# An attention and mixture-of-experts kernel on one Trainium2 core: row stores in four pieces, a weight's quarters further apart, an 80/64 split of the pooled tokens, and an earlier flag

## The chip, the cores and the metric

The kernel runs on one core of one Trainium2 chip. The metric is device time in microseconds of one execution. A core has engines that run side by side, each with its own queue of instructions: TensorE (PE, with its weight loads shown as PEld), VectorE (DVE), ScalarE (ACT), GpSimd (POOL) and SyncE (SP), which here does nothing but issue DMA transfers. An engine takes its instructions in the order in which the program lists them; semaphores make one wait for another.

## The reference

Eight batches, eight heads, 576 tokens, head size 64. Two attentions are added: one over tokens pooled by four (144 of them), whose output is repeated four times, and one over a band of tokens less than four apart. The sum, seen as 4608 rows of 512, goes through a mixture of eight experts: each row goes to the one expert with the largest logit.

```python
q_d = q.reshape(B, H, Sd, factor, D).mean(axis=3)      # k_d, v_d too
out_up = np.repeat(sm_attn(q_d, k_d, v_d), factor, axis=2)
mask = np.abs(pos[:, None] - pos[None, :]) < factor
out_local = softmax(where(mask, scale * q @ k.T, -1e9)) @ v
x = (out_up + out_local).transpose(0, 2, 1, 3).reshape(B * S, H * D)
logits = normalized(x) @ normalized(expert_emb).T / tau
expert_idx = np.argmax(logits, axis=1)
for e in range(E):
    h = np.maximum(x[expert_idx == e] @ w1[e], 0.0)
    out[expert_idx == e] = gate_w[expert_idx == e, None] * (h @ w2[e])
```

## The kernel before, in words

**Attention.** The work is cut into 32 units, each a pair of heads of one batch (four units to a batch). A loop over iterations -2 to 32 (`attention`) goes through a hand-written list of small operations, ORDER, in each iteration; LEAD says for each operation by how many units it runs ahead. In iteration i, k and q of unit i + 2 are transposed (L373), the scores of unit i + 1 are made (its mask matmul is L418, so that the mask of unit u marks iteration u - 1), and unit i is finished: its value matmuls (`op_val`, L522, 36 of them as PE counts) and pooled values (`op_vald`, L509). Unit i - 1 is turned into rows (`op_xr`).

**Pooled values.** The 144 pooled tokens lie on partitions, in two groups CD = (128, 16). `load_v` (L348) loads v for both groups, `op_pv` and `op_vd` (L409, L414, on POOL) add four rows to one, `op_wdT` and `op_adT` bring the pooled attention to the same shape, `op_vald` multiplies the two groups one after the other.

**Loads.** All of them are issued by SP, in program order: k and q for two units at a time (`load`, L342, eight transfers), v for one unit (`load_v`, two), and vw, the overlapping windows of v that the banded attention needs, for two units, a "half" (`load_w`, L357 and L363: two edge transfers, four middle windows, two edge transfers). Half j serves units 2j and 2j + 1; its vw is listed in iteration 2j - 3 and needed in iteration 2j. One half's eight transfers are what the trace shows as L357 x2, L363 x4, L357 x2.

**Weights of the first expert.** `first_weights` is a generator that moves one step in each iteration whose number less one is in W0, just after the place called mid. It loads w1 in four quarters, squares and splits them into two float16 parts on ACT (L857) and DVE (L858), and loads w2's quarters (L877) into the space that w1's quarters leave: a quarter is asked for right after the split that frees its space, in iterations 10, 11, 12 and 13. Squares of w2 follow in iterations 16 to 18, its splits in 20, 21, 23 and 24.

**Rows and places.** When a batch's four units are done, `place` gives functions that run in the following iterations. `store` (at mid, iteration 4b + 5 for batch b) finishes the logits and writes the batch's 576 rows of 520 values to DRAM (`xd`): four tiles of 128 rows in one transfer (L582) and the last 64 rows in another (L583). `most`, `first` and `count` run at the place called tail of that iteration and the next two; they find the expert of each row and its place in that expert's list. For batch 7 all of it comes after the attention. Early gathers (L1111, POOL, in iteration 28) fetch the first three slots of rows from batches 0 to 5; behind them on POOL stands the pooling of v for unit 29 (L414).

**Experts.** Rows are handled in slots of 128. A slot takes 24 matmuls with w1 (L1214 to L1216) and 24 with w2 (L1250 to L1252). `run_slots` interleaves slot q's first half with slot q - 1's second half. Where the next slot has another expert, `renew` splits new weights under a branch on ACT, DVE and POOL; later matmuls wait for that branch, taken or not. `out_rows` (L1259, ACT) scales a slot's result, `store` (L1263, POOL) scatters it. After the last of the 38 fixed slots, `last_slots` loads a flag into a register on every engine (L1091) and branches on it: five more slots are run if the flag is set, and it is not with these inputs.

Of the kernel before, what the change touches and what calls it, by code (L numbers as in the profile page):

```python
# [8 lines left out]
F32 = mybir.dt.float32  # L9
# [13 lines left out]
SD = S // 4  # L23
G, QB = S // 64, 32
WK, WV = QB + 6, 64 + 6
CD = (128, SD - 128)
CP = S // 6
TB = 128
NTB = -(-S // TB)
# [27 lines left out]
MASKED = -1.0e30  # L57
KSC, QSC = 2.0 ** -2, 2.0 ** -5

W0 = (-1, 0, 1, 2, 4, 5, 6, 7, 8, 9, 10, 11, 12, 15, 16, 17, 18, 19, 20, 22, 23)  # L60


class Kern:
# [128 lines left out]
    def attention(self, ctx):  # L192
# [7 lines left out]
        for i in range(2):  # L200
# [3 lines left out]
            self.an.append(z.tile([128, G, WV], F32, name=f"an{i}"))  # L204
            self.sums.append(z.tile([128, G + 3], F32, name=f"sums{i}"))
            self.vw.append(z.tile([WV, G, 4, D], F32, name=f"vw{i}"))
        self.vr = [z.tile([128, 2, 2, 4 * D], F32, name=f"ld_v{i}") for i in range(3)]
        self.lg = z.tile([TB, NTB, E + 1], F32, name="lg")
        self.oh = self.cp.tile([TB, B, NTB + 1, E], BF16, name="oh")
        units = [(b, hp) for b in range(B) for hp in range(NHP)]  # L210
# [32 lines left out]
            nc.vector.memset(self.xT[i][:, S:], 0.0)  # L243
            nc.vector.memset(self.sums[i], 1.0)
        for vr in self.vr:
            nc.gpsimd.memset(vr[:, 1], 0.0)
        next(crows)
        load(1)
        load_v(0)
# [159 lines left out]
        self.nc.gpsimd.tensor_tensor(out=vr[:, :, 0:2 * D], in0=vr[:, :, 0:2 * D], in1=vr[:, :, 2 * D:], op=ALU.add)  # L409

    def op_vd(self, s):
        v, vd = s["v"], self.wk.tile([128, 2, 2, D], F32, name="vd")
        s["vd"] = vd
        self.nc.gpsimd.tensor_tensor(out=vd, in0=v[:, :, :, 0:D], in1=v[:, :, :, D:2 * D], op=ALU.add)  # L414

# [82 lines left out]

    def op_adT(self, s, c):
        if "adT" not in s:  # L500
            s["adT"] = self.wk.tile([128, 2, 2, 3, 48], F32, name="adT", bufs=1)
        self.nc.scalar.activation(out=s["adT"][:CD[c], c].rearrange("p h c j -> p c h j"),
                                  in_=s["wdT", c].rearrange("p c (h j) -> p c h j", h=2), func=AF.Copy)

# [65 lines left out]
    def place(self, b, xr, ls, mid):  # L570

        nc, rt = self.nc, self.rt
        v = nc.vector
        lg, oh = self.lg, self.oh[:, b]
        shp = [TB, NTB, E]

        def bc(x):
            return x.unsqueeze(2).broadcast_to(shp)

        def save(queue):  # L580
            r0 = b * S
            queue.dma_start(out=self.xd[r0:r0 + S - TR].rearrange("(t p) c -> p t c", p=TB), in_=xr[:, :NTB - 1])  # L582
            queue.dma_start(out=self.xd[r0 + S - TR:r0 + S], in_=xr[:TR, NTB - 1])  # L583

        def store():
            pt = self.bank()[:, :NTB * 32].rearrange("p (t e) -> p t e", e=32)
            nc.tensor.transpose(out=pt[:, :NTB - 1], in_=ls[:, :TB], identity=self.ident)
            nc.tensor.transpose(out=pt[:TR, NTB - 1], in_=ls[96:, TB:], identity=self.ident[96:, 96:])
            for ps, ts in ((slice(0, TB), slice(0, NTB - 1)), (slice(0, TR), slice(NTB - 1, NTB))):
                v.tensor_scalar(out=lg[ps, ts, :E], in0=pt[ps, ts, :E], scalar1=self.itau[ps], scalar2=None, op0=ALU.mult)  # L590
            v.tensor_copy(out=xr[:, :, DM:], in_=lg[:, :, :E])
            save(nc.sync)

        def most():

            l8 = lg[:, :, :E]
            mx = s["mx"] = rt.tile([TB, NTB], F32, name="lmx")
            v.reduce_max(out=mx, in_=l8, axis=AX.X)
            v.tensor_tensor(out=l8, in0=l8, in1=bc(mx), op=ALU.is_ge)

        def first():

            l8, mx = lg[:, :, :E], s["mx"]
            v.tensor_tensor(out=l8, in0=l8, in1=self.rev, op=ALU.mult)
            v.reduce_max(out=mx, in_=lg, axis=AX.X)
            v.tensor_tensor(out=oh[:, :NTB], in0=l8, in1=bc(mx), op=ALU.is_equal)

        def count():

            pk = self.bank()[:, :(NTB + 1) * E].rearrange("p (t e) -> p t e", e=E)  # L610
            nc.tensor.matmul(out=pk, lhsT=self.tri, rhs=oh, start=True, stop=False)
            for t in range(1, NTB + 1):
                nc.tensor.matmul(out=pk[:, t:], lhsT=self.onesb, rhs=oh[:, :NTB + 1 - t], start=False,
                                 stop=(t == NTB))
            rk = rt.tile(shp, F32, name="rk")
            pos = s["pos"] = rt.tile([TB, NTB], F32, name="pos")
            v.tensor_tensor(out=rk, in0=pk[:, :NTB], in1=self.base.unsqueeze(1).broadcast_to(shp), op=ALU.add)
            v.tensor_tensor(out=self.base, in0=self.base, in1=pk[:, NTB], op=ALU.add)
            v.tensor_tensor(out=rk, in0=rk, in1=oh[:, :NTB], op=ALU.mult)
            v.reduce_sum(out=pos, in_=rk, axis=AX.X)  # L620

        def divide():

            pos, posi = s["pos"], rt.tile([TB, NTB], I32, name="posi")
            v.tensor_copy(out=posi, in_=pos)
            v.tensor_scalar(out=posi, in0=posi, scalar1=SLOT - 1, scalar2=None, op0=ALU.bitwise_and)
            pm, pb = self.pm[:, b], self.pb[:, b]
            v.tensor_copy(out=pm, in_=posi)
            v.tensor_tensor(out=pb, in0=pos, in1=pm, op=ALU.subtract)
            for t in range(NTB):  # L630
                nc.gpsimd.tensor_scalar(out=self.at[:, b * NTB + t], in0=self.iota, scalar1=pm[:, t:t + 1],
                                        scalar2=None, op0=ALU.is_equal)

        def pick():
            most()
            first()

        def rank():
            count()
            divide()  # L640

        s = {}
        if b == B - 1:
            return [store, pick, rank]
        mid.append(store)
        return [most, first, rank] if b >= BEARLY - 1 else [most, first, count, divide]

# [218 lines left out]
    def first_weights(self):  # L866
# [6 lines left out]
        def get(which, p):  # L873
            w = (self.w1, self.w2)[which][0].rearrange("(c p) f -> p c f", p=128)
            src = self.piece(w, which, p)
            t = flat[:, p].rearrange("p (c f) -> p c f", c=src.shape[1])
            nc.sync.dma_start(out=t, in_=src)  # L877
            return t
# [23 lines left out]
        yield  # L902
        for p in range(NP):
            split(0, p)
            tiles[p] = get(1, p)
            yield
        square(1, 0, 1)
        yield
        square(1, 2)
# [94 lines left out]
        with tc.If(code > 4 if which else code < 1):  # L1004
            self.measure(which)

    def run_slots(self, q0, q1):

        last = q1 - 1
        for q in range(q0, q1):  # L1010
# [50 lines left out]
            self.weigh(q)  # L1061
            if ahead:
                self.turn(q + 2)
            if ps:
                self.out_rows(q - 1, ps)
            if q > q0 + 1:
                self.stage_next(1, b - 1, 1)
            self.gate(q)
            if old:
                self.renew(1, b)  # L1070
            if new:
                self.norms(q + 1)
# [3 lines left out]
            if old:  # L1076
                self.stage_next(1, b, *((0,) if new else (0, 1)))
        self.scale_gate(last)
        self.mm2(last)
        self.store(last)  # L1080

# [6 lines left out]
    def last_slots(self):  # L1088

        q0, q1 = NEARLY + NFIX, NEARLY + NSLOT  # L1090
        more = self.nc.values_load(self.flg[:1, NFIX, 3:4], min_val=0, max_val=1)  # L1091
        with self.tc.If(more > 0):
            for q in range(q0, min(q0 + 4, q1)):
                self.gather(q)
            for b in (NFIX, NFIX + 1):
# [171 lines left out]
    def run(self):  # L1267
# [80 lines left out]
            yield from w1  # L1348

        self.late = late()  # L1350
        self.run_slots(NEARLY, NEARLY + NFIX)
        self.last_slots()


# [43 lines left out]
```

## Time and profile before

| | us |
|---|---|
| three runs | 730.84, 736.08, 740.85 (median 736.08) |
| profiled execution | 733.08 |
| its span, first to last instruction | 731.4 |
| TensorE busy in it | 701.0 |
| VectorE, ScalarE, GpSimd busy | 473.1, 462.0, 443.4 |
| mean granted TensorE clock | 0.988 |

The profile is of one execution. In a timeline row stand the start in us from the span's beginning, the duration, the engine (with a q where it is the engine's sequencer, as for all transfers that SP issues), the line, the operation, what it writes and reads, its shape, how many were merged, and in brackets the idle time ahead of it and what ended that. A row with a source line has shortest, median and longest duration in ns. In a group the number after the bar is the time busy, then the mean of one in ns, then the idle time ahead.

### The profile page before, as it was taken

Reading aid. Unit: us, or ns where it says so; the run is one execution under the profiler, and the core shown is the slowest. Engines: PE = TensorE matmul, PEld = TensorE weight load, DVE = VectorE, ACT = ScalarE, POOL = GpSimd, SP = SyncE. Lnnn points to the kernel's source line nnn. Section 1 sums busy time; section 2 is a strip of 40 time slices with the busy share of each in tenths; the row PEclk is TensorE's granted clock in tenths of the full one; section 3 lists DMA queues with packets and bytes.
Section 4 is the critical chain, followed back from the end, with each engine's and each line's share of the span. In section 5 each row is a group of like instructions: output and inputs, shape, how many; then the busy total and the mean of one; then the engine's idle time right before and its main releaser. Section 6 shows DMA issues by size and latency. Waiting matters only on the chain. (4 is left out here: it accounts for less than half of the span.)

```text
span 731.4 us, 22049 instructions
## 1 busy us (share of the span) xinstructions
PE 701.0 (96%) x7471; PEld 412.9 (56%) x7471; DVE 473.1 (65%) x1415; ACT 462.0 (63%) x1063; POOL 443.4 (61%) x857
## 2 busy tenths in 40 slices
PE   8999999989999989999999999999999999999992
PEld 5777887768878864444444444444444444444440
DVE  6778799958998887576556467565643565366320
ACT  4677788667787664356666577775755555558420
POOL 5865788765878885556564564556466645564420
PEclk9999999989999999999999999999999999999997
DMA  9889889988788976959959988898897599779640
GB/s 162 163 202 193 221 185 234 211 210 213 158 215 185 215 244 129 221 123 248 235 126 250 231 208 216 191 247 193 251 220 132 116 238 216 147 175 202 177 74 19
DMA packets 284117, 138.92 MB, mean 190 GB/s; under 512 B 251186, under 2 KB 260402, under 8 KB 283968
## 3 DMA queue, kind: packets, MB, share of 16 engines
q1 hardware_dynamic: 277248, 118.15, 73.8%
q0 software_dynamic: 6560, 19.03, 8.2%
q8 instruction: 61, 1.00, 0.6%
q14 instruction: 88, 0.72, 0.3%
q10 hardware_dynamic: 160, 0.02, 0.0%
HBM read 213.05 MB, written 20.33 MB: 319 GB/s over the span
## 5 line engine op out<-in xcount | busy, mean ns | idle before, releaser
L1214 PE MATMUL bank<-w1h,xT 128*128 128x512 f16 x328 | 124.3, 379 | 1.4 <-ACTq L995 1.4
L1250 PE MATMUL bank<-w2h,hT 128*128 128x512 f16 x328 | 124.4, 379 | 0.9 <-ACTq L995 0.9
L1215 PE MATMUL bank<-w1l,xT 128*128 128x512 f16 x328 | 124.3, 379 | 0.1
L1252 PE MATMUL bank<-w2h,hT 128*128 128x512 f16 x328 | 124.4, 379 | 0.0
L1251 PE MATMUL bank<-w2l,hT 128*128 128x512 f16 x328 | 124.4, 379 | 0.0
L1216 PE MATMUL bank<-w1h,xT 128*128 128x512 f16 x328 | 124.3, 379 | 0.0
L1111 POOL DMA_INDIRECT xg<-xd,ids x41 | 45.8, 1118 | 79.7 <-POOLq L995 36.9
L1227 ACT ACTIVATE h<-bank 128x512 f16<-128x512 f32 x82 | 48.3, 589 | 58.4 <-PE bank L1216 57.5
L1263 POOL DMA_INDIRECT out_dram<-o,ids x41 | 44.9, 1096 | 50.0 <-ACTq L995 20.0
L380 ACT ACTIVATE kq<-bank 128x288 f32<-128x288 f32 x128 | 48.1, 472 | 38.8 <-PE bank L373 38.4
L833 ACT ACTIVATE junk<-st 128x1024 bf16<-128x1024 f32 (+1 forms) x30 | 67.5, 2251 | 4.6 <-DVE end L734 2.7
L1259 ACT ACTIVATE o<-bank,gt 128x512 f32<-128x512 f32 x41 | 27.8, 677 | 63.5 <-issue 18.7
L409 POOL TENSOR_TENSOR ld_v<-ld_v 128x256 f32<-128x256 f32 x64 | 48.9, 783 | 22.6 <-DMA ld_v<-in_v_dram 22.6
L389 POOL TENSOR_TENSOR pool_kq<-kq 128x288 f32<-128x288 f32 x62 | 45.3, 731 | 25.1 <-ACT kq L380 25.1
L81 POOL TENSOR_SCALAR nw_t<-nw_y,nw_a 128x1 f32<-128x1 f32 x123 | 51.7, 420 | 12.4
L1231 DVE SCALAR_TENSOR_TENSOR h<-bank,h 128x512 f16<-128x512 f32 x82 | 56.3, 688 | 2.7 <-ACTq L1004 2.2
L858 DVE SCALAR_TENSOR_TENSOR w2l<-st,wscl,w2h 128x1024 f16<-128x1024 f32 x32 | 39.6, 1280 | 26.1 <-ACT w2h L857 26.1
L1214 PEld LDWEIGHTS <-xT 128*128 128x128 f16 x328 | 35.1, 107 | 34.5 <-DMA xT<-x 0.5
L1251 PEld LDWEIGHTS <-hT 128*128 128x128 f16 x328 | 32.0, 98 | 39.4 <-issue 1.2
L1250 PEld LDWEIGHTS <-hT 128*128 128x128 f16 x328 | 32.0, 98 | 39.0 <-DMA hT<-h 0.6
L1216 PEld LDWEIGHTS <-xT 128*128 128x128 f16 x328 | 31.9, 97 | 39.1 <-issue 0.4
L1252 PEld LDWEIGHTS <-hT 128*128 128x128 f16 x328 | 32.0, 98 | 38.8
(221 smaller groups left out, 1556.2 us busy)
## 6 DMA issues: line engine op xcount, KB each, us to landing
st<-in_moe_w_dram SPq DMA_DIRECT2D x148, 1024.0 KB
ld_k<-in_k_dram SPq DMA_DIRECT2D x64, 144.0 KB
ld_q<-in_q_dram SPq DMA_DIRECT2D x64, 144.0 KB
xd<-xr SPq DMA_DIRECT2D x8, 1040.0 KB
ld_v<-in_v_dram SPq DMA_DIRECT2D x32, 256.0 KB
st<-in_moe_w_dram SPq DMA_DIRECT2D x16, 512.0 KB
vw<-in_v_dram SPq DMA_DIRECT2D x64, 122.5 KB
vw<-in_v_dram SPq DMA_DIRECT2D x32, 64.0 KB
```

What stands on the lines that cost most here:

```text
L81: g.tensor_scalar(out=t, in0=y, scalar1=y, scalar2=a, op0=ALU.mult, op1=ALU.mult)
L380: self.nc.scalar.activation(out=dst, in_=s["qk", r, w].rearrange("p (m i) -> p i m", m=3), func=AF.Copy, scale=(KSC, QSC)[w])
L409: self.nc.gpsimd.tensor_tensor(out=vr[:, :, 0:2 * D], in0=vr[:, :, 0:2 * D], in1=vr[:, :, 2 * D:], op=ALU.add)
L833: self.nc.scalar.activation(out=junk, in_=src, func=AF.Square, accum_out=acc)
L1214: nc.tensor.matmul(out=ps, lhsT=xT[:, 0, k], rhs=self.w1h[:, k, ns], start=(k == 0), stop=False)
L1215: nc.tensor.matmul(out=ps, lhsT=xT[:, 0, k], rhs=self.w1l[:, k, ns], start=False, stop=False)
L1216: nc.tensor.matmul(out=ps, lhsT=xT[:, 1, k], rhs=self.w1h[:, k, ns], start=False, stop=(k == self.KC - 1))
L1227: self.nc.scalar.activation(out=h2[:, 0], in_=ps, func=AF.Relu)
L1231: self.nc.vector.scalar_tensor_tensor(out=h2[:, 1], in0=ps, scalar=0.0, in1=h2[:, 0], op0=ALU.max, op1=ALU.subtract)
L1250: nc.tensor.matmul(out=ps, lhsT=hh, rhs=self.w2h[:, j, :], start=(j == 0), stop=False)
L1251: nc.tensor.matmul(out=ps, lhsT=hh, rhs=self.w2l[:, j, :], start=False, stop=False)
L1252: nc.tensor.matmul(out=ps, lhsT=hl, rhs=self.w2h[:, j, :], start=False, stop=(j == self.FC - 1))
```

## The change

CD becomes (80, 64); the tiles that hold it have 80 partitions instead of 128. `save` writes only a range of row tiles, always on SP's queue: for batches 0 to 6 tile 0 goes at `store`, tile 1 at `most`, tile 2 at `first`, and tile 3 with the last 64 rows at `count`. Batch 7 is stored as before. w2's quarters are asked for in iterations 10, 12, 13 and 15; its squares come in iterations 17, 19 and 21, its splits in 23 to 26. In the last slot of `run_slots` the renewal of w2 stands ahead of `out_rows` of the slot before. The flag is loaded ahead of the last slot's second half, by a function handed to `run_slots`.

```diff
-CD = (128, SD - 128)
+CD = (80, SD - 80)
...
-W0 = (-1, 0, 1, 2, 4, 5, 6, 7, 8, 9, 10, 11, 12, 15, 16, 17, 18, 19, 20, 22, 23)
+W0 = (-1, 0, 1, 2, 4, 5, 6, 7, 8, 9, 10, 11, 12, 14, 16, 18, 20, 21, 22, 23, 24, 25)
...
-        self.vr = [z.tile([128, 2, 2, 4 * D], F32, name=f"ld_v{i}") for i in range(3)]
+        self.vr = [z.tile([CD[0], 2, 2, 4 * D], F32, name=f"ld_v{i}") for i in range(3)]
...
-            nc.gpsimd.memset(vr[:, 1], 0.0)
+            nc.gpsimd.memset(vr[CD[1]:, 1], 0.0)
...
-        def save(queue):
+        def save(t0, t1):
             r0 = b * S
-            queue.dma_start(out=self.xd[r0:r0 + S - TR].rearrange("(t p) c -> p t c", p=TB), in_=xr[:, :NTB - 1])
-            queue.dma_start(out=self.xd[r0 + S - TR:r0 + S], in_=xr[:TR, NTB - 1])
+            if t0 < NTB - 1:
+                n = min(t1, NTB - 1)
+                nc.sync.dma_start(out=self.xd[r0 + t0 * TB:r0 + n * TB].rearrange("(t p) c -> p t c", p=TB),
+                                  in_=xr[:, t0:n])
+            if t1 == NTB:
+                nc.sync.dma_start(out=self.xd[r0 + S - TR:r0 + S], in_=xr[:TR, NTB - 1])
...
-            save(nc.sync)
+            save(0, 1 if b < B - 1 else NTB)
...
+            if b < B - 1:
+                save(1, 2)
...
+            if b < B - 1:
+                save(2, 3)
...
+            if b < B - 1:
+                save(3, NTB)
...
         for p in range(NP):
             split(0, p)
-            tiles[p] = get(1, p)
+            if p != 1:
+                tiles[max(p - 1, 0)] = get(1, max(p - 1, 0))
             yield
+        tiles[NP - 1] = get(1, NP - 1)
+        yield
...
-    def run_slots(self, q0, q1):
+    def run_slots(self, q0, q1, end=None):
...
+            if old and not new:
+                self.renew(1, b)
             if ps:
                 self.out_rows(q - 1, ps)
...
-            if old:
+            if old and new:
                 self.renew(1, b)
...
         self.scale_gate(last)
+        if end:
+            end()
         self.mm2(last)
...
-        more = self.nc.values_load(self.flg[:1, NFIX, 3:4], min_val=0, max_val=1)
-        with self.tc.If(more > 0):
+        with self.tc.If(self.more > 0):
...
+        def more():
+            self.more = self.nc.values_load(self.flg[:1, NFIX, 3:4], min_val=0, max_val=1)
+
-        self.run_slots(NEARLY, NEARLY + NFIX)
+        self.run_slots(NEARLY, NEARLY + NFIX, more)
```

More of the change, by code (lines that the diff above doesn't have):

```diff
@@ L411, in op_vd @@
     def op_vd(self, s):
-        v, vd = s["v"], self.wk.tile([128, 2, 2, D], F32, name="vd")
+        v, vd = s["v"], self.wk.tile([CD[0], 2, 2, D], F32, name="vd")
         s["vd"] = vd
@@ L500, in op_adT @@
         if "adT" not in s:
-            s["adT"] = self.wk.tile([128, 2, 2, 3, 48], F32, name="adT", bufs=1)
+            s["adT"] = self.wk.tile([CD[0], 2, 2, 3, 48], F32, name="adT", bufs=1)
         self.nc.scalar.activation(out=s["adT"][:CD[c], c].rearrange("p h c j -> p c h j"),
```

## The prediction

> **What bounds the kernel now.** I read the page first, then the busy times by stage, then the rows around the one stage in which TensorE (PE) falls behind, then the end.
>
> ```profile
> span 731.4 us, 22049 instructions
> PE 701.0 (96%) x7471; PEld 412.9 (56%) x7471; DVE 473.1 (65%) x1415; ACT 462.0 (63%) x1063; POOL 443.4 (61%) x857
> ```
> ```profile
> 90.00:140.00 50.00, 49.93 (x1084) 40.13 (x1082) 47.35 (x114) 39.16 (x124) 41.88 (x61) 1.00 0.89 211
> 140.00:160.00 20.00, 16.82 (x319) 13.42 (x318) 12.15 (x31) 13.63 (x42) 12.14 (x22) 0.85 0.94 213
> 160.00:180.00 20.00, 20.00 (x377) 16.02 (x376) 15.77 (x45) 15.38 (x52) 13.92 (x24) 0.98 0.87 198
> 160.00:240.00 80.00, 79.73 (x1666) 64.44 (x1665) 70.25 (x174) 61.64 (x198) 61.26 (x94) 1.00 0.84 193
> ```
>
> PE is the bound: 701 of 731.4 us. The columns of the stages are the stage, its length, then PE, PEld, DVE, ACT and POOL busy, granted clock, DMA share and GB/s. In the attention PE is full in 90:140 and 160:240, but from 140 to 160 it loses 3.2 us, and there alone the clock is under 1. Half speed for 0.15 x 20 / 0.5 = 6.0 us of that stage and 0.02 x 20 / 0.5 = 0.8 us of the next one makes 6.8 us. The mask matmul, one per unit (a pair of heads of a batch), gives the price:
>
> ```profile
> 145.33 0.31 PE L418 MATMUL bank<-mask,identb 128*128 128x342 bf16 x1
> 157.96 0.49 PE L418 MATMUL bank<-mask,identb 128*128 128x342 bf16 x1
> 167.10 0.31 PE L418 MATMUL bank<-mask,identb 128*128 128x342 bf16 x1
> 237.23 0.31 PE L418 MATMUL bank<-mask,identb 128*128 128x342 bf16 x1
> ```
>
> The nine units from 167.10 to 237.23 take 70.13 / 9 = 7.79 us each; the two before take 12.63 and 9.14. So the stall costs 12.63 + 9.14 - 15.58 = **6.2 us**, about half of it idle time and half the half clock behind it. What ends it is the load of vw, the windows of v:
>
> ```profile
> 143.58 0.57 SPq L582 DMA_DIRECT2D xd<-xr  x1
> 144.19 2.13 SPq L583 DMA_DIRECT2D xd<-xr  x1
> 146.42 0.61 SPq L877 DMA_DIRECT2D st<-in_moe_w_dram  x1
> 147.13 1.12 SPq L357 DMA_DIRECT2D vw<-in_v_dram  x2
> 148.30 4.25 SPq L363 DMA_DIRECT2D vw<-in_v_dram  x4
> 152.65 0.63 SPq L357 DMA_DIRECT2D vw<-in_v_dram  x1
> 213.26 2.93 SPq L363 DMA_DIRECT2D vw<-in_v_dram  x4
> ```
> ```profile
> 149.95 0.86 PE L509 MATMUL bank<-adT,vd 128*64 128x144 f32 x8 [0.61 <-ACT adT L502]
> 153.34 0.56 PE L522 MATMUL bank<-aT,vw 70*64 70x64 f32 x6 [1.95 <-DMA vw<-in_v_dram]
> ```
>
> Batch 2's store (L582, L583), the last quarter of w2 (L877) and the vw load for units 16 and 17 ("half 8") stand one behind the other on SP's queue. SP goes from one transfer to the next with some 0.05 us between them, so it is never ahead: a load is issued when SP gets to it. That is the second bound of this stage.
>
> **The change, part by part.**
>
> *Store in pieces, quarters apart.* The large transfer of a store carries four of a batch's four and a half row tiles:
>
> ```profile
> xd<-xr SPq DMA_DIRECT2D x8, 1040.0 KB
> ```
>
> So batch 2's store put 1040 x 4.5 / 4 = 1170 KB on the queue ahead of half 8's load, and the four quarters of w2 had been asked for in four units running. Afterwards 520 KB of the store and three quarters stand ahead of it, and all of both ahead of half 9's load. Bytes and descriptors are the same in the end, so what counts is how much earlier SP gets through, and how much room PE has behind it. Room is read from vw loads: SP's last issue of one, its landing, and the matmuls that need it.
>
> ```profile
> 86.02 1.15 SPq L357 DMA_DIRECT2D vw<-in_v_dram  x2
> 184.80 1.41 SPq L357 DMA_DIRECT2D vw<-in_v_dram  x2
> 216.28 1.15 SPq L357 DMA_DIRECT2D vw<-in_v_dram  x2
> ```
> ```profile
> 88.71 0.34 PE L522 MATMUL bank<-aT,vw 70*64 70x64 f32 x4 [0.42 <-DMA vw<-in_v_dram]
> 187.81 1.27 PE L522 MATMUL bank<-aT,vw 70*64 70x64 f32 x36
> 219.29 1.27 PE L522 MATMUL bank<-aT,vw 70*64 70x64 f32 x36
> ```
>
> Half 4 waited until 88.71 for a transfer whose issue ended at 87.17: landing takes 1.54 us. The last four of a unit's 36 value matmuls need it, some 1.0 us behind the first. Half 10 (SP done at 186.21, landed 187.75, needed 188.8) has 1.1 us of room, half 12 (217.43, 218.97, 220.3) has 1.3. So even with the stall gone PE cannot come more than about 1.1 us earlier through the later units, unless SP does. SP comes earlier by what the burst cost it: L583 took 2.13 us where its other rows have 0.52 (below), and half 8's four middle windows 4.25 where half 12's took 2.93, of which I take 1.0: together 2.6 us.
>
> Against that, each batch has five transfers instead of two, three more for SP.
>
> ```profile
> L583 SPq DMA_DIRECT2D xd<-xr x8: 514/519/2130, 79.6 to 282.8; - x8
> ```
>
> One more costs SP between 0 (it fills a pause that SP would have had anyway, such as the 2.13 here) and 0.52 + 0.06 = 0.58 us. DMA engines are busy 0.84 to 0.94, which argues for pauses, but SP has no gap even at 0.84, which argues for the full price; I take 0.25, a little under the middle. Ahead of half 10 stand three more transfers for each of batches 0 to 2, ahead of half 12 those of batch 3 too. Gain at half 10: 1.1 + 2.6 - 9 x 0.25 = 1.45; at half 12: 1.3 + 2.6 - 12 x 0.25 = **0.9 us**, the smaller, which I take. By the ends: 0 gives 3.7, 0.58 gives 3.9 - 7.0 = -3.1. At half 8 itself the need was near 152.4 (153.34 - 1.95 + 1.0) and the landing 153.80 + 1.54 = 155.3: short by 2.9. SP's 2.6 and one quarter fewer (0.5), less 6 x 0.25, leave it short by about 1.3, too little, I think, to halve the clock. The stall is late next at halves 9, 10 and 12, in small pieces.
>
> [...]
>
> *The last piece of batch 5.* Early gathers read batches 0 to 5. Its store was issued in iteration 25; its last piece now stands in iteration 27, just ahead of half 15's load.
>
> ```profile
> 249.63 1.13 SPq L357 DMA_DIRECT2D vw<-in_v_dram  x2
> ```
> ```profile
> 252.98 1.27 POOL L1111 DMA_INDIRECT xg<-xd,ids  x1 [0.73 <-DVE ids L700]
> 257.19 0.74 POOL L414 TENSOR_TENSOR vd<-ld_v 128x256 f32<-128x256 f32 x1
> ```
> ```profile
> 257.99 0.47 PE L509 MATMUL bank<-adT,vd 128*64 128x144 f32 x4
> ```
> ```profile
> DMA to landing us min/median/max: 2.6/4.7/8.0
> ```
>
> Two issues from 249.63 on end near 250.8; landing, by the gathers' own (the row above), takes 2.6 or more, so 253.4 at best and 255.5 by the median. The first gather starts at 252.98. Behind it on POOL stand two gathers and vd of unit 29, done at 257.93, and PE needs that at 257.99: no room. Cost 0.4 to 2.5 us, and more if SP is later; I take **1.0**, towards the low end, as a plain store lands without the gather's reading of ids.
>
> *80 and 64 tokens.* The same number of instructions with the same free size:
>
> ```profile
> L409 POOL TENSOR_TENSOR ld_v<-ld_v 128x256 f32<-128x256 f32 x32 | 25.2, 788 | 22.1 <-DMA ld_v<-in_v_dram 22.1
> L409 POOL TENSOR_TENSOR ld_v<-ld_v 16x256 f32<-16x256 f32 x32 | 24.9, 779 | 0.5 <-DMA ld_v<-in_v_dram 0.5
> ```
>
> 128 and 16 partitions cost 788 and 779 ns, so any split does; bytes stay. Zero.
>
> *w2's squares and splits later.* The last split moves from iteration 24 to 26, the same sixteen instructions.
>
> ```profile
> L858 DVE SCALAR_TENSOR_TENSOR w2l<-st,wscl,w2h 128x1024 f16<-128x1024 f32 x32 | 39.6, 1280 | 26.1 <-ACT w2h L857 26.1
> ```
>
> DVE is busy 70.25 of 80 us in 160:240, with the splits in it; four units running have 1.28 us each where there were two pairs. Between 0 and 0.7 us (two units, 7.79 x 0.88 + 1.28 less 7.79); I take 0, since they lie behind PE's own 7.79.
>
> *The end.* In the last fixed slot the check on w2 stood on ACT behind out_rows, which waits for the slot before.
>
> ```profile
> 710.62 0.38 PE L1251 MATMUL bank<-w2l,hT 128*128 128x512 f16 x1
> 710.84 0.38 PE L1252 MATMUL bank<-w2h,hT 128*128 128x512 f16 x1
> 712.09 0.38 PE L1250 MATMUL bank<-w2h,hT 128*128 128x512 f16 x1 [0.87 <-ACTq L995]
> ```
> ```profile
> 711.30 0.69 ACT L1259 ACTIVATE o<-bank,gt 128x512 f32<-128x512 f32 x1 [4.07 <-issue]
> ```
> ```profile
> L1091 POOLq TENSOR_LOAD <-flg x1: 287/287/287, 718.3 to 718.3; - x1
> ```
>
> PE's matmuls follow each other at 0.22 us, so the last 24 could start at 711.06, not 712.09: **1.03 us**. ACT idles 4.07 us ahead of L1259; the moved check fits there, and without that cover it would cost what it costs now. The flag's load leaves the chain of POOL behind the last store: 0 (if the store's landing sets the end) to 0.29; I take all. On PE it now stands ahead of the last 24 matmuls, hidden by those already queued. Sum at the end: **1.3 us**, bounds 0 and 1.3.
>
> **Sum.** 733.1 (the profiled execution; 731.4 of span and 1.7 around it) - 0.9 + 1.0 + 0 + 0 - 1.3 = 731.9. That execution is 3.0 us under the median of 736.1 and inside the three runs (730.84 to 740.85). What lifts a run above it is, I think, a stall like this one, and smaller bursts make those rarer, so I carry the sum over as it is: **732 us**.
>
> **Rivals.**
> 1. *All of the stall goes and nothing is given back* (0.20): 733.1 - 6.2 - 1.3 = 725.6. For it: 6.2 us stand in one place. Against it: 1.1 us of room at half 10.
> 2. *SP's issue becomes the bound; slower* (0.25): each transfer costs SP its full 0.58 us and vw comes late at every second half: 3.1 later at half 12, 1.0 at the gathers or 3 with SP's lateness, 1.3 won: 733.1 + 2.8 to 4.8, 737. It decides from 12c - 3.9 + 1.0 - 1.3 > 0, c over 0.35 us. For it: SP without gaps. Against it: its pauses.
> 3. *A smaller stall still halves the clock* (0.10): 6.8 / 2 = 3.4 more than my sum, 735.3.
> 4. *The check does not free PE at the end* because another wait ends last there (0.05): 733.2.
>
> **How the numbers follow.** My forecast has 0.40. The range reaches from rival 1, less a little for the runs' spread, to rival 2 with the median's 3 us on top: **724 to 740**. A measurement of this kernel tells about 2% from no change, 721.4 or 750.8; all cases lie inside, so faster 0.05, same 0.92, slower 0.03.
>
> **What would show it.** Right: no unit over 10 us in the mask rows; clock 1.00 in 140:180; waits of L522 on vw in pieces under 1.5 us around halves 9 to 12; L1111 first ended by xd, not ids; the last 24 matmuls without a gap. Wrong: unit 17 still over 12 us; SP with gaps (then the pieces are free, rival 1); or units 18 to 28 over 8.1 us each (rival 2).

## The result, and the profile after

The kernel after takes 742.57 us (median of 20 runs, 739.60 to 748.26), the kernel before on the same chip 734.38 (20 runs, 730.84 to 740.85): a ratio of 1.0107, 95% interval [1.0088, 1.0127]. The change costs some 8 us. It was forecast to gain one; the range ended at 740. The profiled execution of after is its slowest, 748.26, so its single losses are larger than those of a usual run. Losses below are read from profiles, sizes from medians. Runs more than 1.5% above the fastest of their kernel are left out of every ratio; one of 1877.98 us, of the kernel with the ratio 0.9959, is among them.

The head of the page of after, and the busy times of the same stages as before (stage, length, then PE, PEld, DVE, ACT, POOL busy, granted clock, DMA share, GB/s):

```profile
span 746.5 us, 22071 instructions
...
PE 706.2 (95%) x7471; PEld 418.6 (56%) x7471; DVE 471.6 (63%) x1415; ACT 463.4 (62%) x1063; POOL 446.6 (60%) x857
```
```profile
90.00:140.00 50.00, 46.29 (x944) 37.77 (x941) 41.92 (x103) 34.70 (x106) 38.48 (x56) 0.93 0.89 198
140.00:160.00 20.00, 20.00 (x406) 16.10 (x405) 16.58 (x43) 15.02 (x52) 14.85 (x26) 1.00 0.84 187
160.00:180.00 20.00, 13.24 (x257) 10.74 (x255) 9.88 (x24) 9.76 (x29) 11.06 (x18) 0.77 0.80 199
160.00:240.00 80.00, 73.24 (x1514) 59.29 (x1515) 61.37 (x154) 58.30 (x185) 54.52 (x83) 0.94 0.85 197
```

The stage that lost 3.2 us before, 140:160, is now full, at clock 1.00: the stall at half 8 is gone in this execution. In its place PE loses 3.7 us in 90:140 and 6.8 us in 160:180, each with a granted clock of 0.50 from within the wait on, 102.3 to 109.2 and 170.6 to 180.8. The mask rows, one a unit, show the two places, and what PE waited for:

```profile
91.42 0.31 PE L418 MATMUL bank<-mask,identb 128*128 128x342 bf16 x1
103.01 0.45 PE L418 MATMUL bank<-mask,identb 128*128 128x342 bf16 x1 [3.23 <-DVE ls L568]
113.53 0.31 PE L418 MATMUL bank<-mask,identb 128*128 128x342 bf16 x1
...
160.18 0.31 PE L418 MATMUL bank<-mask,identb 128*128 128x342 bf16 x1
175.01 0.44 PE L418 MATMUL bank<-mask,identb 128*128 128x342 bf16 x1 [6.41 <-DVE ls L568]
185.37 0.31 PE L418 MATMUL bank<-mask,identb 128*128 128x342 bf16 x1
```

Units of 11.59 and 10.52 us, 14.83 and 10.36, where 7.79 is usual: (22.11 - 15.58) + (25.19 - 15.58) = 16.1 us. Unit 30, under "Open" at the end of the section on the prediction, loses another 4.2. The DVE copy L568 is not the cause; it waits in its turn, 9.01 us in the second case. ScalarE's timeline has the first engine that stands still:

```profile
102.11 0.28 ACT L554 ACTIVATE xr<-bank 128x128 f32<-128x128 f32 x1 [4.62 <-DMA xd<-xr]
...
174.11 0.28 ACT L554 ACTIVATE xr<-bank 128x128 f32<-128x128 f32 x1 [7.60 <-DMA vw<-in_v_dram]
```

L554 is the first write of a batch's rows, and the row buffer `xr` has two buffers. Batch 2 writes where batch 0's rows lie, batch 4 where batch 2's do. With the store in pieces, the last piece of batch b is listed in iteration 4b + 7, and batch b + 2 writes in 4b + 9. SP runs some two iterations behind the list, as its timeline shows (L584 is the store of whole tiles, L587 that of the last 64 rows):

```profile
96.83 0.62 SPq L584 DMA_DIRECT2D xd<-xr  x1
97.49 0.51 SPq L587 DMA_DIRECT2D xd<-xr  x1
...
167.21 0.57 SPq L887 DMA_DIRECT2D st<-in_moe_w_dram  x1
167.82 0.47 SPq L584 DMA_DIRECT2D xd<-xr  x1
168.33 0.51 SPq L587 DMA_DIRECT2D xd<-xr  x1
```

Batch 0's last piece leaves SP at 98.00 and ScalarE goes on at 102.11, 4.1 us later; batch 2's leaves at 168.84, and ScalarE goes on at 174.11. In the second row the page names a vw transfer, but L554 reads or writes nothing of vw. The trace has the last packet of the store's last two transfers end at 101.36 in the first case and at 173.39 in the second, each shortly ahead of L554. Everything behind L554 on ScalarE, the copies of k and q (L380) among it, waits; then PE, DVE and POOL do.

The end went as forecast. Of the last matmuls with w2 the 24 that stood behind a gap of 0.87 us now follow without one:

```profile
727.27 0.38 PE L1268 MATMUL bank<-w2h,hT 128*128 128x512 f16 x1
727.49 0.38 PE L1266 MATMUL bank<-w2h,hT 128*128 128x512 f16 x1
727.70 0.38 PE L1267 MATMUL bank<-w2l,hT 128*128 128x512 f16 x1
```

From the last unit's mask (277.46) to the end of the span it takes 469.0 us, 470.4 before (731.4 - 261.00). All of the loss stands in the attention.

### The profile page after: what moved, and what is told of

It reads as the page before. It is cut to its first block, busy times and chain, and to the rows that moved or that the text cites. A ratio compares the mean times of both kernels' runs of the same rounds, so it can differ in the third digit from the quotient of the medians.

```text
span 746.5 us, 22071 instructions
## 1 busy us (share of the span) xinstructions
PE 706.2 (95%) x7471; PEld 418.6 (56%) x7471; DVE 471.6 (63%) x1415; ACT 463.4 (62%) x1063; POOL 446.6 (60%) x857
## 5 line engine op out<-in xcount | busy, mean ns | idle before, releaser
L380 ACT ACTIVATE kq<-bank 128x288 f32<-128x288 f32 x128 | 47.8, 474 | 33.8 <-PE bank L373 32.9
L81 POOL TENSOR_SCALAR nw_t<-nw_y,nw_a 128x1 f32<-128x1 f32 x123 | 54.2, 440 | 12.4
L409 POOL TENSOR_TENSOR ld_v<-ld_v 80x256 f32<-80x256 f32 x64 | 50.4, 807 | 15.3 <-DMA ld_v<-in_v_dram 15.3
L491 ACT ACTIVATE aT<-bank 70x384 f32<-70x384 f32 x96 | 43.8, 489 | 18.7 <-PE bank L484 18.3
L1266 PEld LDWEIGHTS <-hT 128*128 128x128 f16 x328 | 32.1, 98 | 40.7 <-DMA hT<-h 2.6
L1268 PEld LDWEIGHTS <-hT 128*128 128x128 f16 x328 | 32.1, 98 | 38.7
```

Source lines behind the costliest of these rows:

```text
L81: g.tensor_scalar(out=t, in0=y, scalar1=y, scalar2=a, op0=ALU.mult, op1=ALU.mult)
L380: self.nc.scalar.activation(out=dst, in_=s["qk", r, w].rearrange("p (m i) -> p i m", m=3), func=AF.Copy, scale=(KSC, QSC)[w])
L1266: nc.tensor.matmul(out=ps, lhsT=hh, rhs=self.w2h[:, j, :], start=(j == 0), stop=False)
L1268: nc.tensor.matmul(out=ps, lhsT=hl, rhs=self.w2h[:, j, :], start=False, stop=(j == self.FC - 1))
```

## The experiments

Theory at the start, from the rows above: **the row buffer**, ScalarE waits for the late last piece. Rival: **SP's issue**, three more transfers a batch. All ratios are to runs of before on the same chip (735.0 to 735.5 us), with 95% intervals.

### The store alone

Five transfers at once, where `store` stands:

```diff
-            save(0, 1 if b < B - 1 else NTB)
+            for t0, t1 in ((0, 1), (1, 2), (2, 3), (3, NTB)) if b < B - 1 else ((0, NTB),):
+                save(t0, t1)
```

> The changed kernel, but all five transfers of a batch are issued together at store (iteration 4b + 5), none later. Row-buffer theory (the last pieces are listed in iteration 4b + 7, SP is some 2.3 iterations late, and ACT's first write into the same row buffer for batch b + 2 in iteration 4b + 9 waits until they have landed): no wait of ACT's L554 over 1 us, time 731 to 736, near before. SP-issue theory (three more transfers a batch hold SP up): the same number of transfers, so the time stays at 740 to 744, with vw loads late.

740.62 us, 1.0076 [1.0041, 1.0111]: the rival's time, though L554 waits for no transfer in its profile. Next, two transfers as before, but both as late as the last piece (`save(0, NTB)` in `count` only):

> The changed kernel, but a batch is stored in two transfers as before, both at count (iteration 4b + 7). Row-buffer theory: as late as the changed kernel's last pieces and more bytes behind each other, so L554 waits 4 to 9 us for batches 2 and 4 and the time is 741 to 748. SP-issue theory: no transfer more than before, so 731 to 736.

742.07 us, 1.0105 [1.0060, 1.0150]: the row buffer's time. Then after with the old store (`save(0, NTB)` at `store`, nothing later), and before with nothing but the spread store:

> The changed kernel with the store of before (two transfers at store); the quarters further apart, 80 and 64 tokens and the edits at the end are kept. Both theories: the loss is gone. The end gives 1.0 to 1.3; if the quarters further apart shorten the stall at half 8 as well, 727 to 731; if not, 732 to 734.

740.31 us, 1.0067 [1.0041, 1.0092].

> The kernel before with nothing but the store in pieces over iterations 4b + 5 to 4b + 7. Row-buffer theory: the whole loss and a little more, since the end's 1.3 us are missing: 741 to 746, with L554 waiting on DMA at batch 2 or 4. If the moved quarters or the 80/64 split had a part in the loss, it is under 739.

737.66 us, 1.0034 [1.0006, 1.0062].

This points to lateness and not to number, without proving it: both transfers late against both at once is 1.0105 against 1.0067, five at once against two at once 1.0076 against 1.0067, 0.7 us for all of them, though the intervals of both pairs overlap. ScalarE's waits, in the kernel with two late transfers (total us, times, longest):

```profile
ACT xr L554 <- DMA xd<-xr: 9.5, 2, 5.0
```

Here the page names the store itself, twice. But both theories failed on the third kernel: it has the old store and still loses 5 us. Something else in the change costs more than its store.

### One part of the change at a time

The kernel before with one part put in: CD = (80, 64) and its tiles; the later quarters, squares and splits; the two edits of the end. The fourth has the end's edits and the store in three transfers, tiles 0 and 1 at `store` and the rest at `most`:

```diff
-            save(nc.sync)
+            save(0, 2 if b < B - 1 else NTB)
...
             v.tensor_tensor(out=l8, in0=l8, in1=bc(mx), op=ALU.is_ge)
+            if b < B - 1:
+                save(2, NTB)
```

> The kernel before with only the pooled tokens divided as 80 and 64. The old store with the moved quarters, the split and the end's edits was 0.67% slower than before, about 5 us. Theory A, the split makes SyncE slower: in the trace of after the transfer of 64 tokens took SyncE 0.60 us where that of 16 took 0.46, and the one of 80 took 0.32 to 0.55 where that of 128 took 0.39, some 0.2 us a unit, over 30 units 5 to 7 us on a queue that has hardly a gap, so loads come later and matmuls wait: 738 to 742 on a chip where before takes 735. Theory B, the moved quarters are to blame: the split alone costs nothing that shows, 734 to 737.

742.42 us, 1.0095 [1.0061, 1.0130]: **the split alone makes as much of a loss as the whole change.**

> The kernel before with only the second matrix's quarters asked for further apart and its splits put into later iterations. Theory B: the last splits now stand in units 27 and 28, VectorE and GpSimd run there side by side, L473 takes 1.8 us in place of 1.0 and TensorE waits 1.4 us for it; unit 28 takes 9.6 us in place of 7.7, and unit 30, which lost 3 to 4 us to gaps in L426 in all three kernels that had the moved quarters and the split, loses them here too: 738 to 741. Theory A (the split is to blame): 734 to 737, and unit 28 takes 7.7 us.

736.32 us, 1.0033 [0.9998, 1.0068], with unit 28 at 9.37 us: theory A's time with theory B's slow unit 28, while unit 30 loses nothing (7.84 us). The expected rows are there. DVE, POOL and PE of this kernel, and the same step of DVE and POOL before:

```profile
237.52 1.76 DVE L473 TENSOR_TENSOR an<-a,sums 64x342 f32<-64x342 f32 x2
```
```profile
237.26 0.74 POOL L414 TENSOR_TENSOR vd<-ld_v 128x256 f32<-128x256 f32 x1
237.97 0.93 POOL L389 TENSOR_TENSOR pool_kq<-kq 128x288 f32<-128x288 f32 x1
```
```profile
239.43 0.84 PE L484 MATMUL bank<-ident,an 128*70 128x128 f32 x5 [1.06 <-DVE an L473]
```
```profile
236.55 1.03 DVE L473 TENSOR_TENSOR an<-a,sums 64x342 f32<-64x342 f32 x2
```
```profile
235.48 0.74 POOL L414 TENSOR_TENSOR vd<-ld_v 128x256 f32<-128x256 f32 x1
237.63 0.67 POOL L389 TENSOR_TENSOR pool_kq<-kq 128x288 f32<-128x288 f32 x1 [1.42 <-ACT kq L380]
```

Before, POOL was idle while L473 ran, and two of them took 1.03 us. Here POOL works right through, and they take 1.76. The whole profile of before has 64 L473: the 20 that ran with POOL idle throughout took 0.51 us each, the eleven that overlapped POOL's L414 0.72 to 0.97, and the 33 beside other work of POOL 0.50 to 1.27. But the quarters are not needed for it: with the split alone unit 28 takes 9.26 us too; its v comes late there (POOL waits 1.78 us for it), POOL then works beside L473, and two of these take 2.49 us.

> The kernel before with only the two edits of the end (check placed ahead of the last expert's scale, flag loaded sooner). By the prediction's term and the trace of after, whose last 24 matmuls have no gap: 1.0 us of gap and 0.3 us of flag load gone, 733.5 to 734.5 on a chip where before takes 735, and all else unchanged. If it is slower than before, a longer program or a moved instruction costs time in the attention, and part of the loss has nothing to do with any of the four parts.

734.41 us, 0.9998 [0.9969, 1.0028]: the interval holds both the 1.3 us and nothing. Taken alone, split, quarters and end would add up to 1.0126; the kernel with all three and the old store had 1.0067. So the parts do not simply add, and a part's size holds only for the pair of kernels from which it is read.

> The end's edits, and the rows stored in two pairs of transfers: 128-token pieces 0 and 1 where the store stands, the rest one unit later. No quarters moved, no split. Theory of the row buffer: the last piece is asked for two units sooner than in after, so it has landed before the batch after next writes the buffer; ScalarE's L554 waits on no transfer, and the 12.6 us unit at half 8 is gone as in after: 726 to 732. Rival, any spreading of the store costs SyncE time: 735 to 738, with loads late in other units.

732.43 us, 0.9950 [0.9918, 0.9982]: faster than before. But the edit does not do what was expected of it. `most` runs at the tail of the same iteration as `store`, so that SP issues all three transfers behind each other:

```profile
76.47 1.10 SPq L584 DMA_DIRECT2D xd<-xr  x2
77.61 0.86 SPq L587 DMA_DIRECT2D xd<-xr  x1
78.58 1.82 SPq L357 DMA_DIRECT2D vw<-in_v_dram  x2
```

Only at batch 2 another transfer, a quarter of w2, stands between them. The rows are stored in one burst, nearly as before, and where an expectation below speaks of rows over two units, it means this burst. Where the gain over before comes from is not shown: the end's edits alone have 0.9998, their interval overlaps, and in the profiled execution the last unit's mask stands at 261.75, in before's at 261.00.

L554 waits for no transfer here; these are all of its waits in the attention of this kernel, both for PE, and the same two stand in the profile of before:

```profile
ACT xr L554 <- PE bank L559: 2.4, 1, 2.4
...
ACT xr L554 <- PE bank L509: 0.9, 1, 0.9
```

What was expected of half 8 did not come, as the burst is still there: in the profiled execution PE waits 3.90 us there for vw, more than before, and unit 17 takes 14.06 us. In the profiles of the 17 kernels in which SP issues all loads, unit 17 takes 9.6 to 14.1 us in twelve, and 7.7 to 8.5 in five. Four of the five are those whose last transfer is listed in iteration 4b + 7: after, the two late transfers, the spread store alone, and after without the split (below). The same four, and no others, have L554 waiting for a transfer; with it, units 10 and 11 lose 4.8 to 6.8 us not long before. Whether the later store or this delay of PE makes the room at half 8, no run separates.

### What the split costs by

Two ways are open: SP takes longer to issue the two transfers, or the DMA engines take longer to move them. A third, the arithmetic, is settled by the profiles, in mean ns of one, before and with the split: POOL's additions L409 793 and 783, then 796 and 794; PE's L509 311 and 307, then 311 and 308; ScalarE's L502 383 and 399, then 392 and 403.

> The kernel before, its 128 pooled tokens fetched by two transfers of 64 in place of one of 128; the tokens, the bytes, the descriptors and all arithmetic stay as they are. Theory A (SyncE's own time is the price of the split): two transfers of 64 take SyncE some 1.1 us in place of 0.4, so 0.7 us more a unit, which is three times the 0.2 us that 80 and 64 add: clearly slower, 750 us or more where before takes 735. Rival (the arithmetic on 80 and 64 partitions, or how the descriptors fall on the 16 engines, is the price): within 0.5% of before.

Edit: `for c, p0, n in ((0, 0, 64), (0, 64, 64), (1, 0, SD - 128))`. 756.27 us, 1.0299 [1.0265, 1.0333]. SP's time alone can do it, if there is enough of it.

> The kernel before with the pooled tokens divided as 72 and 72, both halves and both heads fetched by one transfer of 288 descriptors of 1 KB. Theory A: one transfer must take SyncE less than the 0.85 us of the two, 0.5 to 0.6 us by the rows of 64 and 80, so 0.25 us a unit comes back to SyncE, loads are early, and the time is 728 to 733 where before takes 735. Rival (a more even division of the arithmetic, or of the descriptors, is the price): 738 to 742, as with 80 and 64.

```diff
+        src = self.v[b, 2 * hp:2 * hp + 2].rearrange("h (c i r) d -> i (h c) (r d)", c=2, r=4)
+        self.nc.sync.dma_start(out=vr.rearrange("p h c x -> p (h c) x"), in_=src)
```

741.37 us, 1.0097 [1.0062, 1.0132]. SP's theory fails here: the one transfer takes SP 0.37 us in place of 0.95, and the kernel is as slow as with 80 and 64. The source line of v before, with the split, and with one transfer (shortest, median, longest ns):

```profile
L348 SPq DMA_DIRECT2D ld_v<-in_v_dram x64: 384/420/1821, 12.5 to 255.9; - x64
```
```profile
L348 SPq DMA_DIRECT2D ld_v<-in_v_dram x64: 312/601/1407, 12.3 to 259.5; - x64
```
```profile
L345 SPq DMA_DIRECT2D ld_v<-in_v_dram x32: 300/372/1102, 12.3 to 258.6; - x32
```

SP's queue of the DMA engines from 20 to 256 us (packets, MB, share of the time of 16 engines): before, split alone, three transfers, one transfer.

```profile
q1 hardware_dynamic: 121069, 46.47, 86.4%
```
```profile
q1 hardware_dynamic: 118687, 45.86, 90.9%
```
```profile
q1 hardware_dynamic: 113150, 42.92, 79.7%
```
```profile
q1 hardware_dynamic: 118445, 45.94, 94.8%
```

Share x 16 x 236 us over the packets gives the mean time of one: 26.9 ns before, 28.9 with the split, 26.6 with three transfers, **30.2** with one. So three transfers load SP and leave the packets alone; one transfer spares SP itself and lengthens the packets, and SP's other transfers take longer to issue, as if SP waited for the engines: its k and q rows (the same 112) took 109.5 us, against 86.5 before. The packets of 1 KB alone, which are the pooled tokens, took 55.0, 62.0, 57.4 and 69.0 ns in these four profiles. To take SP out of it, ScalarE's queue issued the pooled tokens, undivided and divided:

```diff
-            self.nc.sync.dma_start(out=vr[:n, c], ...
+            self.nc.scalar.dma_start(out=vr[:n, c], ...
```

> The kernel before with the pooled tokens' two transfers issued by ScalarE's queue in place of SyncE's; split, store and quarters as before. SyncE gets back 0.95 us a unit, ScalarE (178 of 236 us busy in the attention) has as much more to issue. If SyncE's own time sets the loads: faster, 725 to 732 where before takes 735. If the 16 DMA engines (88% busy in the attention) set them: within 0.5% of before, with longer packets.

784.78 us, 1.0657 [1.0604, 1.0710].

> As the kernel with ScalarE's queue, but with the tokens divided as 80 and 64, so that the split's longer issue is on ScalarE and not on SyncE. Theory A (the split costs by SyncE's issue time): equal to that kernel within 0.4%. Theory C (the split costs by packets that take longer: the 1 KB ones took 62 ns in place of 55 and the 256-byte ones 22.8 in place of 21.3 with it): slower than that kernel by 0.6 to 1.2%, with the same longer packets.

787.52 us, 1.0705 [1.0662, 1.0747]. Dividing costs 0.45% here, with overlapping intervals, and so between what the two theories gave. As times both are a miss: ScalarE stands still until POOL has freed the buffer that the transfer writes, in the first of them four times, 24.3 us in all and up to 6.4 at a time:

```profile
ACT xr L551 <- POOL vd L414: 24.3, 4, 6.4
```

(L551 is only the next instruction behind the two transfers.) But these transfers have a queue of their own here, q10, and it shows their packets alone, undivided and divided:

```profile
q10 hardware_dynamic: 8000, 7.38, 10.6%
```
```profile
q10 hardware_dynamic: 7680, 7.08, 12.8%
```

10.6% x 3776 us / 8000 = 50.0 ns, 12.8% x 3776 / 7680 = **62.9 ns** a packet, for the same bytes a packet and the same issuer. (A tenth of them have 4 bytes; those of 1 KB alone took 54.6 and 68.7 ns.) Dividing the tokens as 80 and 64 makes their packets 26% longer. The 1 KB packets on SP's queue went the same way, from 55.0 ns with 128 and 16 partitions to 62.0 with 80 and 64 and 69.0 with 72. Fewer partitions a transfer cannot be all of it: none of the three transfers writes more than 64, and their packets took 57.4 ns, hardly more than the 55.0 of before. Why dividing lengthens the packets, no run shows.

How much is SP's part? Three transfers in each fourth unit only (`hp == 0`) add SyncE time of about the split's size:

> As the kernel with three transfers a unit for the pooled tokens (3.0% slower than before), but only in each fourth unit, so that SyncE's added time is about that of the split, some 0.2 us a unit on average, with packets of the old length. Theory A (SyncE's issue time is the split's price): 0.6 to 0.9% slower than before, 739 to 742 where before takes 735. Theory C (the longer packets are its price, and SyncE has room for 0.2 us a unit): within 0.3% of before, 733 to 737.

```profile
q1 hardware_dynamic: 118536, 45.70, 84.0%
```

738.00 us, 1.0036 [1.0009, 1.0063], with packets of 26.8 ns. Between the two expectations. By the trace SP spent 38.2 us on 30 units' v here, 1.27 a unit, against 0.95 before and 1.13 with the split (29.4 us in 31 units, 34.0 in 30). So 0.32 us a unit cost 0.36%, and 1.05 us a unit cost 3.0% in the kernel with three transfers everywhere. The split's 0.18 us a unit is then worth 0.2 to 0.5%, by proportion to the one and to the other, an estimate; the rest of its 0.95%, about half or more, is put down to the longer packets by subtraction; no run has the longer packets alone at a usual pace.

### Putting after together without what costs

> The kernel after with the pooled tokens left at 128 and 16. If the split is the cause of the loss in after: 733 to 738 where before takes 735 (store spread +0.3%, quarters +0.3%, end -0.1%, and the stall at half 8 gone). If the parts stand for themselves and the row buffer's wait is what costs most: 740 to 744, as after.

737.41 us, 1.0030 [1.0004, 1.0057]. The row buffer's wait is still there: the profile has L554 held three times by transfers, 11.4 us in all.

> As the kernel with the rows stored over two units (0.995 of before), but the second pair is asked for one unit later still, one unit ahead of the last piece of after. Row buffer: by the traces SyncE runs some 2.3 units behind the list and the piece lands 4 to 5 us after its issue, so it lands about when ScalarE's L554 of the batch after next comes: L554 waits 0 to 3 us in one or two batches, 733 to 738 where before takes 735. Rival (a later piece only spares SyncE): 730 to 733, as with one unit.

733.88 us, 0.9985 [0.9949, 1.0021]; L554 waits for no transfer. So the last piece may come in iteration 4b + 6, and not in 4b + 7. This is the kernel whose rows are really stored over two units: in its profile batch 0's first transfer is issued at 78.33 and its second at 85.95. Its time cannot be told from that of the end's edits alone (0.9998), so no run shows a gain from spreading the store, even without the wait.

> The kernel after without the split and with the rows in two pairs of transfers, the second one unit after the first; the quarters moved as in after and the end's edits in. If the parts add up (rows over two units with the end 0.995, quarters 1.003): 0.998, 732 to 736 where before takes 735, with no wait of L554 on a transfer and unit 28 at 9.3 to 9.7 us. If the moved quarters bring a gain once the row buffer's wait is gone: under 732.

731.58 us, 0.9959 [0.9934, 0.9983]: after without the split and with its store in a burst of three transfers beats both kernels, like the other kernel with that burst (0.9950). The two intervals overlap almost wholly, so moving the quarters brings nothing and costs nothing that shows there; that the time lies 0.4 us under the expectation's mark for a gain says nothing at this spread. Units 17 and 28 still take 11.62 and 9.58 us. One step at a time, 1.0107 becomes 1.0030 without the split, and 0.9959 with the last piece two units sooner: 0.77% and 0.71%, 5.7 and 5.2 us. The second step also has three transfers a batch for five, and both carry a part of unit 30, which takes 11.67, 9.07 and 7.83 us in the three profiles. Against the store of before the late pieces cost less: 0.34% alone, and 0.40% from the kernel with the old store (1.0067) to after.

> The end's edits, the rows stored over two units, and the pooled tokens by one transfer of 72 and 72; the quarters where they were. Theory A: the gains of the one transfer and of the store over two units (0.5%) come together, 722 to 729 where before takes 735. Rival: 736 to 742, the even division spoils what the store gains.

738.00 us, 1.0044 [1.0019, 1.0069]: the rival's range. The even division costs here what it costs alone, 0.94% and 0.97%.

> The end's edits and the rows stored over two units, with the pooled tokens (128 and 16) issued by ScalarE's queue. If SyncE's time sets the loads, the gains add: 719 to 728 where before takes 735. If the DMA engines do: 730 to 735.

778.12 us, 1.0587 [1.0538, 1.0636]: ScalarE waits as in the other kernels with its queue, and nothing can be read from it on SP.

## Why the prediction was wrong

Its forecast, 732, stood 10.6 us below the median, and on the wrong side. Its base, 733.1, is 1.3 us under the median of before (734.38); the rest lies in the steps:

- *What bounds the kernel.* Right in the main: PE is full, and of the losses above all but unit 30's are a late load or a wait and the half clock that came with it. The granted clock was 0.50 for 6.8 us in the attention of before (153.8 to 160.7), and for 6.8, 6.8, 10.2 and 3.4 us in that of after. The sum took small stalls to be too little to halve the clock, and that was wrong: the first 6.8 us of after begin at 54.5, behind waits of PE of 0.29 and 0.54 us for vw. With only the quarters moved, two waits at half 3 (unit 6) are followed by a stage at clock 0.57:

```profile
72.09 1.03 PE L522 MATMUL bank<-aT,vw 70*64 70x64 f32 x26 [0.48 <-DMA vw<-in_v_dram]
...
73.62 0.34 PE L522 MATMUL bank<-aT,vw 70*64 70x64 f32 x4 [0.50 <-DMA vw<-in_v_dram]
```
```profile
74.00:78.00 4.00, 4.00 (x90) 3.40 (x91) 2.22 (x4) 2.65 (x6) 3.19 (x5) 0.57 0.81 185
```

Half speed for 0.43 x 4 / 0.5 = 3.4 us. So what rival 3 supposed did come behind smaller stalls. Its 3.4 us, half of the 6.8, was an estimate for which before has no stretch of that length; the runs had 3.4 in one case and 6.8 in another. Nor did each small wait bring it: in before PE waited 0.89 and 0.54 us for DVE ahead of the matmuls at 270.2 and 271.6, and the clock stayed at 1.00. What decides it, no run shows.

- *Store in pieces, -0.9.* At half 8 unit 17 takes 7.69 us where it took 12.63, but only in company with the row buffer's wait ahead of it, so the smaller burst cannot be credited with it. The price of one more transfer, 0.25 us in a range from 0 to 0.58, looks too high: by the ratios 21 of them cost 0.7 us in all, with intervals of some 2.5 us to either side. What the step left out is the wait that it added. It named two effects of a later piece, the loads behind it and the gathers, and not the third: **the buffer that the piece reads stays occupied until the piece has landed** (last packets at 101.36 and 173.39, ScalarE on at 102.11 and 174.11). The first row write of the batch after next, L554, stood in the trace of before without a wait for a transfer, two iterations behind the new last piece; SP's lag of two iterations could be read from the same rows. Against the burst of three transfers that is 0.71%; against the store of before the step costs 0.34 to 0.40%, 2.5 to 2.9 us, where it was forecast to gain 0.9.
- *Last piece of batch 5, +1.0.* It did not come. The first gather starts at 265.28 with 0.53 us of idle time, ended by ids, not by the rows.

```profile
265.28 1.28 POOL L1127 DMA_INDIRECT xg<-xd,ids  x1 [0.53 <-DVE ids L710]
```

- *80 and 64 tokens, zero.* **The step that failed most:** 0.77 to 0.95%, 5.7 to 7.0 us. It looked at POOL's additions, where 128 and 16 partitions cost the same, and concluded "any split does; bytes stay". It did not price the two transfers. By the medians SP takes 0.48 and 0.61 us for 80 and 64 tokens, 0.39 and 0.46 for 128 and 16, and the packets are longer. DMA engines at 0.84 to 0.94 stood in the quoted rows, and with them the warning that a longer packet is paid.
- *w2's squares and splits later, 0 to 0.7.* 0.33% [-0.02, 0.68] alone, nothing that shows in the kernel with 0.9959. Of its bounds the working had only DVE's load; that two L473 take 1.76 us where POOL works beside them, and 1.03 with POOL idle, was not in it.
- *The end, -1.3.* Supported by the profiles (no gap; from the last mask on 467.2 to 469.0 us in eight profiles with the end's edits and 472.0 and 475.5 in two, 469.3 to 471.3 in six without them and 474.9 in one); the runs alone cannot tell it from nothing.
- *Rivals.* Rival 2 gave 737 for SP's issue as the bound. The sign was right, and the spread store alone came to 737.66, but with the row buffer's wait in its profile (7.2 us of L554). Its mechanism is real in one part that it did not name, the split.
- The signs listed as right (no unit over 10 us, clock 1.00 in 140:180) failed: units 5, 10, 11, 18, 19 and 30 took over 10 us, and the clock was 0.77 in 160:180. The list had no row for a wait of ScalarE. It watched the loads and not who waits for the stores.

Had the forecast been for the kernel without the split and with the last piece two units sooner, 0.9959, it would have been good to 0.3%: 732.0 / 733.1 is 0.9985. That would have been luck in part, since the stall at half 8, on whose end the store's term rests, is still there in that kernel.

**Open.** Unit 30 took 11.67 us in after and 7.51 before. In after its 72 matmuls L426 come with gaps for which the page has no cause, and behind them the clock is 0.50 from 269.6 to 273.0:

```profile
266.03 0.93 PE L426 MATMUL bank<-kq 64*32 64x38 f32 x44
...
267.42 0.32 PE L426 MATMUL bank<-kq 64*32 64x38 f32 x8 [0.46 <-issue]
...
268.19 0.38 PE L426 MATMUL bank<-kq 64*32 64x38 f32 x16 [0.45 <-issue]
```
```profile
253.73 0.85 PE L426 MATMUL bank<-kq 64*32 64x38 f32 x72
```

They stand at this place in the profiles of after and of seven other kernels, with the split or without it, where unit 30 takes 9.1 to 12.1 us, and not in the rest; no run was made to tell what TensorE waits for there. Some of what is put down above to the split and the store, where kernels with and without these gaps are compared, may belong here; the kernel with the split alone has none at unit 30, and its 0.95% is free of that. Also not tried: a third row buffer, and so the late piece without its wait.

## What to carry to other kernels

When a store is put off, look for the next writer of the buffer that it reads, count by how many iterations the queue runs behind its list, and keep the store more than that ahead of the writer: here SP ran some two behind, the writer stood in iteration 4b + 9, and in after it waited at two batches for a piece listed in 4b + 7, and with the piece listed in 4b + 6 at none. Price a transfer by its form, too: here the same bytes as 80 and 64 tokens in place of 128 and 16 took SP 1.13 us a unit in place of 0.95 and the DMA engines 28.9 ns a packet in place of 26.9, with SP's queue at 86 to 91% of their time, and the kernel was 0.95% slower with the arithmetic the same. A change of four parts that moves the time by one per cent is to be taken apart part by part before its largest row is believed: here that row was half of the story. Look in the trace, too, whether an edit moved what it was meant to move: here two places in one iteration were taken for two units.

## What the runs showed of the hardware that was not expected

- On a queue of their own, the packets of the same 1 KB rows took 54.6 ns each into 128 and 16 partitions and 68.7 ns into 80 and 64 (50.0 and 62.9 with the queue's 4-byte packets).
- By the medians SP took 0.61 us for a transfer of 64 rows of two heads, 0.46 for one of 16 (0.60 in the kernel with three transfers), 0.39 for one of 128, and 0.37 for one of 72 rows with four pieces each: neither bytes nor rows alone set it.
- With the pooled tokens issued by ScalarE, it stood still up to 6.4 us at a time until POOL had freed the target, and the kernel took 6.6% longer.
- Two DVE instructions L473 took 1.03 us with POOL idle (before) and 1.76 beside it (with only the quarters moved).
